# Attention and two expert layers on one core: side steps between the two layers take other places

## The chip, the cores and the metric

The kernel runs on one core of one Trainium2 chip. The metric is the device time of one execution in microseconds (us); lower is better. Times of the trace are us from the start of the profiled span.

## The reference

A linear attention with a decay for each head (batch 2, 8 heads, 768 steps, 64 channels) gives 1536 token rows of 512. Two layers of experts follow, each with 8 experts of 512 x 1024 and 1024 x 512, in which each token goes to the one expert of its largest logit:

```python
# first layer: tokens with x @ w_skip > 0 only
xc = x[do_compute]
logits = xc @ w_gate
e_idx = np.argmax(logits, axis=1)
...
h = np.maximum(xc[mask] @ w1[e], 0.0)
y[mask] = gate_w[mask, None] * (h @ w2[e])
out[do_compute] = xc + y
# second layer: all tokens, at most capacity rows to an expert, in order of tokens
h = np.maximum(np.einsum('ecd,edf->ecf', disp, w1), 0.0)
y = np.einsum('ecf,efd->ecd', h, w2)
out[i] = gate_w[i] * y[expert_idx[i], pos[i]]
```

So the result of the first layer decides to which expert of the second layer a row goes.

## The kernel before

The kernel has an order written out by hand: each engine does its instructions in the order in which the code issues them. Four stages follow each other. Attention runs in six chunks of 128 steps. The first expert layer (weights `w1a`, `w2a`) has for each expert one block of 128 rows. Then comes a passage, in which expert 0 of the second layer (`w1b`, `w2b`) is done in two blocks of 128 rows, since the first of them is known early. Last come experts 1 to 7 of the second layer, each with a pair of blocks.

Products are of float32 split in two parts: `hi` is a rounded copy that ScalarE makes (L252 for weights, 128 x 1024 a piece), `lo` is the rest that VectorE makes (L255). Three products hi x hi, hi x lo, lo x hi give one. In `layer1` and `layer2` a group is six such products of 512 columns (L794); `layer2` is a generator of four groups for the eight blocks of 128 of its middle dimension, and yields after each.

Beside the products runs side work, one step after a group. `step_side()` moves each generator of the list `side` by one step, and then `pump`s: a piece of weights is split (so many as `pieces[0]` says) and loads are issued from SyncE's queue. `site()` does the same for the list `sited`, without a pump. The side work is `route_b`, which routes finished rows of the first layer to experts of the second:

- step 1: the rows are turned by TensorE (L870) and copied by ScalarE (`x2t`, L871);
- step 2: logits (L875), copied by ScalarE (`lgs`, L877);
- step 3: their sum (L881), and on VectorE the choice of the expert (`pick`, from L301 to `m` in L317) and the gate;
- step 4, the rank: how many rows ahead went to the same expert (L329, L330 on TensorE), then on VectorE L901, L903 and the table `whereb` (L907) that holds the slot of each row;
- step 5, the slots: TensorE adds the row numbers to the slots (L343, into `tab`).

The rows of experts 0 to 5 are routed in couples, those of experts 6 and 7 one by one; the couple of experts 4 and 5 is the third couple here, and the generator for expert 7 is called `last`. Ahead of routing, `result` makes the row of an expert (L849 on VectorE, from the accumulator of `layer2`), and within it `write_rows` (L355, from ScalarE's queue) writes the rows to a table in DRAM. When the last slots are known, VectorE casts them to `ids_b` (L1075), and GpSimd gathers the rows of a block from the table (L362). `turned` turns four blocks of 128 by TensorE (L765), and ScalarE and VectorE split the turned block in `hi` and `lo` (`split`, L378 and L379).

Of the kernel before, what the change touches and what calls it, by code (L numbers as in the profile page):

```python
# [16 lines left out]
NT, DM, E, FF = B * S, H * D, 8, 1024  # L17
# [3 lines left out]
FT = FF // 128  # L21
# [20 lines left out]
def kernel(  # L42
# [132 lines left out]
    def idle(n):  # L175
        for _ in range(n):
            yield
# [567 lines left out]
    def psum(tag="t", bufs=3):  # L745
        return ps.tile([128, 512], F32, tag=tag, bufs=bufs, name=tag)
# [13 lines left out]
    def turned(src, g, tag, divided=True):  # L760

        pool = x_p if tag == "x" else m_p
        t = psum()
        for k in range(4):
            nc.tensor.transpose(t[:, 128 * k:128 * k + 128], src[:, 512 * g + 128 * k:512 * g + 128 * k + 128], ident)  # L765
        t = t.rearrange("p (k t) -> p k t", k=4)
        if divided:
            w = 128 if tag == "x" else 256
            hi = pool.tile([128, 4, w], F32R, tag=tag + "h", name=tag + "h")[:, :, 0:128]
            lo = pool.tile([128, 4, w], F32R, tag=tag + "l", name=tag + "l")[:, :, 0:128]  # L770
            split(t, hi, lo)
            return hi, lo
        as_is = pool.tile([128, 4, 128], F32, tag=tag + "w", name=tag + "w", bufs=1)
        nc.scalar.activation(out=as_is, in_=t, func=ACTF.Copy)
        return (as_is,)
# [70 lines left out]
    def result(e, xs, acc):  # L846

        r2 = row2[e // 2 % 2][:, e % 2, :]
        nc.vector.scalar_tensor_tensor(  # L849
            out=r2[:, 0:DM], in0=acc, scalar=xs[:, GCOL:GCOL + 1], in1=xs[:, 0:DM], op0=ALU.mult, op1=ALU.add  # L850
        )
        nc.gpsimd.tensor_copy(out=r2[:, IDCOL:IDCOL + 1], in_=xs[:, IDCOL:IDCOL + 1])
        xs_free.append(xs)

    def route_b(es, lead, rest):


        n, e = len(es), es[0]
        r2 = row2[e // 2 % 2][:, e % 2:e % 2 + n, :]
        there = sm.tile([128, n], F32, tag="there", name="there")  # L860
        nc.gpsimd.tensor_scalar(out=there, in0=r2[:, :, IDCOL], scalar1=0.0, scalar2=None, op0=ALU.is_lt)
        rm = sm.tile([128, n, 8], F32, tag=f"rmb{n}", name="rmb")
        for i in range(n):
            nc.gpsimd.tensor_scalar(out=rm[:, i, :], in0=rev, scalar1=there[:, i:i + 1], scalar2=None, op0=ALU.mult)
        yield from idle(lead)
        x2t = m_p.tile([128, 2, KT, 128], F32, tag="x2t", name="x2t", bufs=1)
        for i in range(n):
            xr = psum()
            for k in range(KT):
                nc.tensor.transpose(xr[:, 128 * k:128 * k + 128], r2[:, i, 128 * k:128 * k + 128], ident)  # L870
            nc.scalar.activation(out=x2t[:, i], in_=xr.rearrange("p (k t) -> p k t", k=KT), func=ACTF.Copy)  # L871
        yield
        lg = psum()
        for k in range(KT):
            nc.tensor.matmul(out=lg[32 * k:32 * k + 32, 0:128 * n], lhsT=wgt[:, k, :], rhs=x2t[:, 0:n, k, :], start=True, stop=True)  # L875
        lgs = sm.tile([128, 256], F32, tag="lgs", name="lgs")
        nc.scalar.activation(out=lgs[:, 0:128 * n], in_=lg[:, 0:128 * n], func=ACTF.Copy)  # L877
        yield
        lt = psum()
        for i in range(n):  # L880
            nc.tensor.matmul(out=lt[:, 8 * i:8 * i + 8], lhsT=lgs[:, 128 * i:128 * i + 128], rhs=zsum[:, 8:16], start=True, stop=True)  # L881
        m, weigh = pick(
            lt[:, 0:8 * n].rearrange("p (a j) -> p a j", a=n), n, 1, rm, r2[:, :, GCOL + 1:GCOL + 2], None, e == E - 1
        )
        if e < E - 1:
            weigh()
        if e >= E - 2:
            write_rows(nc.scalar, r2, n)
        rhs = sm.tile([128, n, 2, 8], BF16, tag=f"rhsb{n}", name="rhsb")
        cu = sm.tile([128, n, 8], BF16, tag=f"cu{n}", name="cu")  # L890
        nc.gpsimd.tensor_copy(out=cu[:, 0, :], in_=cumb)
        for i in range(1, n):
            nc.gpsimd.tensor_tensor(out=cu[:, i, :], in0=cu[:, i - 1, :], in1=m[:, i - 1, :], op=ALU.subtract)
        nc.gpsimd.tensor_scalar(out=rhs[:, :, 0, :], in0=m, scalar1=p1, scalar2=None, op0=ALU.mult)
        for i in range(n):
            nc.gpsimd.tensor_scalar(out=rhs[:, i, 1, :], in0=m[:, i, :], scalar1=float(128 * (NTILE + es[i])), scalar2=None, op0=ALU.mult)
        yield from idle(1 + rest)
        rk = psum()
        ranked(rk, lc[:, 1, :], m.rearrange("p n j -> p (n j)"), cu.rearrange("p n j -> p (n j)"))
        pr = sm.tile([128, n, 8], F32, tag=f"prb{n}", name="prb")  # L900
        nc.vector.tensor_tensor(out=pr, in0=rk[:, 0:8 * n].rearrange("p (a j) -> p a j", a=n), in1=m, op=ALU.mult)  # L901
        sl = sm.tile([128, n], F32, tag=f"slb{n}", name="slb")
        nc.vector.tensor_reduce(out=sl, in_=pr, axis=AX.X, op=ALU.add)  # L903
        where = []
        for i in range(n):
            where.append(sm.tile([128, 257], BF16, tag="whereb", name="whereb"))
            nc.vector.tensor_scalar(out=where[i], in0=iota, scalar1=sl[:, i:i + 1], scalar2=None, op0=ALU.is_equal)  # L907
        if e < E - 2:
            write_rows(nc.scalar, r2, n)
        nc.gpsimd.tensor_tensor(out=cumb, in0=cu[:, n - 1, :], in1=m[:, n - 1, :], op=ALU.subtract)  # L910
        yield from idle(3 if e == E - 2 else 1)
        for i in range(n):
            to_slots(where[i], rhs[:, i], 8, 8)
        yield
# [38 lines left out]
    def site():  # L953

        for g in list(sited):
            try:
                next(g)
            except StopIteration:
                sited.remove(g)

    def step_side():
        for g in list(side):
            try:
                next(g)
            except StopIteration:
                side.remove(g)
        pump(1, pieces[0])

    def run(gen):

        while True:
            try:
                next(gen)
            except StopIteration as stop:
                return stop.value
            step_side()
# [3 lines left out]
    x = x0[0]  # L980
# [28 lines left out]
    second = layer2(h0, "w2a", 0)  # L1009
# [5 lines left out]
    x = turned(xs1[1], 0, "x")  # L1015
    acc = run(second)
    then_route(0, acc)
    for e in range(1, E):
        first = layer1(x, "w1a", e)
        if e == 1:  # L1020
            for _ in range(2):
                next(first)
                step_side()
            x = turned(xs1[2], 0, "x")
        h = run(first)
        if e + 4 < E:
            xs1[e + 4] = gather(ids[:, e + 4:e + 5], 1 + NT)
        elif e == 4:
            gather(ids[:, 8:9], 1 + NT, a0)
        turn = split_T(h, FT, "hT", (True, not whole("w2a", e, 1)))  # L1030
        if e > 1:
            second = layer2(hT.pop(e - 1), "w2a", e - 1)
            next(second)
            step_side()
            site()
            x = turned(xs1[e + 1] if e + 1 < E else a0, 0, "x")
            if e == E - 1:

                for _ in range(2):
                    next(second)  # L1040
                    step_side()
                    site()
                    next(turn)
            acc = last_step(second, FT // 2 - (3 if e == E - 1 else 1))
            then_route(e - 1, acc, step_side)
        site()
        hT[e] = run(turn)
    side += sited
    second = layer2(hT.pop(E - 1), "w2a", E - 1)
    for i in range(FT // 2):  # L1050
        next(second)
        pieces[0] = i < 2
        step_side()
    acc = run(second)
    result(E - 1, xs1[E - 1], acc)
    last = route_b([E - 1], 0, 0)

    xs2 = {(0, 0): a0}
# [6 lines left out]
    for i in range(1, 13):  # L1065
        next(first)
        if i % 3 == 0:
            step_side()
        if i in (2, 4, 5, 9, 12):
            next(last)  # L1070
    try:
        next(first)
# [5 lines left out]
    second = layer2(h0, "w2b", 0)  # L1078
    next(second)
    h0.append(turned(h, 1, "hT"))  # L1080
    acc = run(second)
    while side:
        step_side()
    x = turned(xs2[0, 1], 0, "x")
    pieces[0] = 1
    ct = totals([cum[:, 0, :], cumb])

# [56 lines left out]
    second = layer2(h0, "w2b", 0)  # L1144
# [3 lines left out]
    x = pair_T(1)  # L1148
# [4 lines left out]
    for e in range(1, E):  # L1153
# [4 lines left out]
        if e + 1 < E:  # L1158
            x = pair_T(e + 1)
# [198 lines left out]
```

## Time and profile before

| what | us |
|---|---|
| median of 3 runs | 388.11 |
| lowest and highest run | 387.08, 388.33 |
| the profiled execution | 386.85 |
| its span in the trace | 385.1 |
| TensorE (PE) busy in the span | 369.1 |
| VectorE (DVE) busy | 244.3 |
| ScalarE (ACT) busy | 213.7 |
| GpSimd (POOL) busy | 120.8 |

The span is the part of the execution that the trace shows. PE stands for the products and PEld for the weight loads that overlap them; the ends of products are modelled, so an idle time ahead of an instruction is shown shorter than the pause between two products by the time of a product's flow through the array. Busy times of engines overlap, and their sum is no time of the kernel.

### The profile page before, as it was taken

What the parts mean: (1) busy time and instruction counts of PE and PEld (TensorE: products, weight loads), DVE (VectorE), ACT (ScalarE), POOL (GpSimd) and SP (SyncE); (2) the same over time, 40 slices, a digit from 0 to 9 for tenths busy, and PEclk for the clock granted to TensorE, in tenths of its full rate; (3) what the DMA queues carried; (4) which work ended last, traced back from release to release, by engine and by line L of the source; (5) the groups of instructions that cost most, each with busy time, mean ns of one, the idle gap of its engine ahead of it and who ended that gap; (6) DMA issues with size and microseconds to landing.
All of it is one profiled execution on the core that took longest, in us unless ns stands there. A gap on an engine that the chain in (4) does not pass through costs nothing. (4 is left out here: it accounts for less than half of the span.)

```text
span 385.1 us, 6795 instructions
## 1 busy us (share of the span) xinstructions
PE 369.1 (96%) x2642; PEld 311.0 (81%) x2642; DVE 244.3 (63%) x402; ACT 213.7 (56%) x317; POOL 120.8 (31%) x185
## 2 busy tenths in 40 slices
PE   8999999899999999998899999999999999999992
PEld 4788887687687787875578998989989898998981
DVE  3657776489896988997426993646727376383200
ACT  1446564398878777894227773537536455563100
POOL 3677764284060240403251401305022040401102
PEclk9999999999999999999999999999999999999998
DMA  8999975799999999899434794956749387110101
GB/s 299 416 413 406 361 240 191 234 337 401 382 390 399 381 339 358 295 338 335 168 106 141 270 333 141 307 202 200 260 145 337 114 261 263 56 52 11 43 3 43
DMA packets 18128, 95.99 MB, mean 249 GB/s; under 512 B 2401, under 2 KB 2657, under 8 KB 8616
## 3 DMA queue, kind: packets, MB, share of 16 engines
q1 hardware_dynamic: 12196, 80.85, 57.0%
q0 software_dynamic: 3280, 9.76, 8.0%
q10 hardware_dynamic: 2612, 4.86, 3.3%
q8 instruction: 23, 0.38, 0.4%
q14 instruction: 17, 0.14, 0.1%
HBM read 87.03 MB, written 9.48 MB: 251 GB/s over the span
## 5 line engine op out<-in xcount | busy, mean ns | idle before, releaser
L255 DVE TENSOR_TENSOR lo<-big,hi 128x1024 fp32r<-128x1024 f32 (+1 forms) x130 | 151.2, 1185 | 55.6 <-ACT hi L252 55.2
L252 ACT ACTIVATE hi<-big 128x1024 fp32r<-128x1024 f32 (+1 forms) x130 | 128.5, 1017 | 6.0 <-DMA big<-in_w1a_dram 4.2
L788 PE MATMUL s<-xh,lo 128*128 128x256 f32 x224 | 63.5, 283 | 0.0
L787 PE MATMUL s<-xl,hi 128*128 128x256 f32 x224 | 63.5, 283 | 0.0
L786 PE MATMUL s<-xh,hi 128*128 128x256 f32 x224 | 63.4, 283 | 0.0
L924 POOL DMA_INDIRECT out_dram<-y,ixo x16 | 18.6, 1165 | 139.2 <-ACT y L919 137.5
L786 PE MATMUL o<-hi,hTh 128*128 128x512 f32 x112 | 44.2, 395 | 0.0
L788 PE MATMUL o<-hi,hTl 128*128 128x512 f32 x112 | 43.7, 390 | 0.0
L787 PE MATMUL o<-lo,hTh 128*128 128x512 f32 x112 | 43.6, 390 | 0.0
L786 PEld LDWEIGHTS s<-xh,hi 128*128 128x128 f32 x224 | 43.0, 192 | 0.3
L787 PEld LDWEIGHTS s<-xl,hi 128*128 128x128 f32 x224 | 43.0, 192 | 0.3
L788 PEld LDWEIGHTS s<-xh,lo 128*128 128x128 f32 x224 | 43.0, 192 | 0.0
L1118 ACT ACTIVATE hTh<-s 128x512 fp32r<-128x512 f32 x28 | 16.7, 598 | 39.0 <-PE s L788 38.6
L1119 DVE SCALAR_TENSOR_TENSOR hTl<-s,hTh 128x512 fp32r<-128x512 f32 x28 | 19.3, 690 | 28.4 <-ACT hTh L1118 28.4
L919 ACT ACTIVATE y<-o,rowc 128x512 f32<-128x512 f32 (+1 forms) x15 | 10.1, 674 | 45.4 <-issue 29.3
L794 PE MATMUL s<-hi,xh 128*128 128x512 f32 x80 | 32.7, 409 | 1.6 <-DVE xl L379 0.9
L794 PE MATMUL s<-lo,xh 128*128 128x512 f32 x80 | 31.3, 391 | 0.0
L794 PE MATMUL o<-hi,hTh 128*128 128x512 f32 x72 | 29.7, 413 | 0.0
L794 PE MATMUL o<-lo,hTh 128*128 128x512 f32 x72 | 28.2, 391 | 0.0
L794 PE MATMUL s<-hi,xl 128*128 128x512 f32 x80 | 24.9, 393 | 0.0
L788 PEld LDWEIGHTS o<-hi,hTl 128*128 128x128 f32 x112 | 21.0, 188 | 4.4
L787 PEld LDWEIGHTS o<-lo,hTh 128*128 128x128 f32 x112 | 21.1, 188 | 4.2
(162 smaller groups left out, 603.9 us busy)
## 6 DMA issues: line engine op xcount, KB each, us to landing
big<-in_w1a_dram SPq DMA_DIRECT2D x16, 1024.0 KB, 8.2
big<-in_w2a_dram SPq DMA_DIRECT2D x16, 1024.0 KB, 6.8
big<-in_w1b_dram SPq DMA_DIRECT2D x16, 1024.0 KB, 5.2
big<-in_w2b_dram SPq DMA_DIRECT2D x16, 1024.0 KB, 5.4
qk<-in_qkv_dram SPq DMA_DIRECT2D x5, 1024.0 KB, 10.5
big<-in_qkv_dram SPq DMA_DIRECT2D x5, 1024.0 KB, 13.2
table<-rowc ACTq DMA_DIRECT2D x5, 516.0 KB
table<-row ACTq DMA_DIRECT2D x3, 516.0 KB, 5.3
```

The source lines that it names most:

```text
L252: nc.scalar.activation(out=hi[:, k], in_=r3[:, k], func=ACTF.Copy)
L255: nc.vector.tensor_tensor(out=lo[:, k], in0=r3[:, k], in1=hi[:, k].bitcast(F32), op=ALU.subtract)
L786: nc.tensor.matmul(out=acc, lhsT=a[0], rhs=w[0], start=first, stop=False)
L787: nc.tensor.matmul(out=acc, lhsT=a[0], rhs=w[1], start=False, stop=False)
L788: nc.tensor.matmul(out=acc, lhsT=a[1], rhs=w[0], start=False, stop=last)
L794: nc.tensor.matmul(out=acc, lhsT=a, rhs=w, start=first and i == 0, stop=last and i == len(todo) - 1)
L919: nc.scalar.activation(out=y[:, 0:n], in_=acc[:, 0:n], func=ACTF.Copy, scale=xs[:, GCOL + 1:GCOL + 2])
L924: new = nc.gpsimd.indirect_dma_start(out=out[:, :], out_offset=bass.IndirectOffsetOnAxis(ap=ix, axis=0), in_=y, in_offset=None, bounds_che ...
L1118: nc.scalar.activation(out=hi[:, g:g + 2, :], in_=acc, func=ACTF.Relu)
L1119: nc.vector.scalar_tensor_tensor(out=lo[:, g:g + 2, :], in0=acc, scalar=0.0, in1=hi[:, g:g + 2, :].bitcast(F32), op0=ALU.max, op1=ALU.subtract
```

## The change

Five places between the two layers are written in another order; no instruction is added or taken away.

```diff
-        yield from idle(3 if e == E - 2 else 1)
+        yield from idle(1 if e < E - 4 or e == E - 1 else 3)
         for i in range(n):
             to_slots(where[i], rhs[:, i], 8, 8)
...
             then_route(e - 1, acc, step_side)
-        site()
+        if e < E - 1:
+            site()
         hT[e] = run(turn)
     side += sited
...
     for i in range(FT // 2):
         next(second)
         pieces[0] = i < 2
-        step_side()
+        if i < FT // 2 - 1:
+            step_side()
     acc = run(second)
     result(E - 1, xs1[E - 1], acc)
+    step_side()
     last = route_b([E - 1], 0, 0)
...
-        if i in (2, 4, 5, 9, 12):
+        if i in (2, 4, 5, 8, 12):
             next(last)
...
     h0.append(turned(h, 1, "hT"))
+    for _ in range(FT // 2 - 2):
+        next(second)
+        step_side()
+    x = turned(xs2[0, 1], 0, "x")
     acc = run(second)
     while side:
         step_side()
-    x = turned(xs2[0, 1], 0, "x")
```

The first two edits concern the third couple: its rank is no longer issued right after the products of expert 6, but in the side step behind the first group of expert 7, and its slots three side steps after the rank instead of one. On TensorE, in the second product of experts 6 and 7, the place of the rank of the couple (`m`, 128 x 16) reads so (`o` is the accumulator, `row_1153` the row of expert 6):

```order
 L794 MATMUL o<-hi,hTl 128x512 x2
+L794 MATMUL o<-hi,hTh 128x512
+L794 MATMUL o<-lo,hTh 128x512
+L794 MATMUL o<-hi,hTh 128x512
+L794 MATMUL o<-lo,hTh 128x512
+L794 MATMUL o<-hi,hTl 128x512 x2
+L870 MATMUL t<-cs,row_1153 128x128 x4
 L329 LDWEIGHTS lc
 L329 MATMUL t<-m,lc 128x16
```

The first group of expert 7 and the turn of row 6 now stand ahead of the couple's rank; its eight slots, which stood behind that turn, stand behind the rank of row 6, after the fourth group.

With the third edit the row of expert 7 is made ahead of the last side step of that loop. On VectorE, at the end of the first layer (`o` is the accumulator of expert 7, L901 to L907 the slot table of row 6):

```order
+L849 SCALAR_TENSOR_TENSOR row_1153<-o,rowc_106 128x512
 L901 TENSOR_TENSOR prb<-t,m 128x8
 L903 TENSOR_REDUCE slb<-prb 128x1
 L907 TENSOR_SCALAR whereb<-iota,slb 128x257
-L849 SCALAR_TENSOR_TENSOR row_1153<-o,rowc_106 128x512
```

The row moved ahead of the three instructions of the slot table. The fourth edit puts the rank of row 7 two products of the first expert's first half sooner, ahead of the turn of `h` on TensorE, and so L901 to L907 of row 7 ahead of the split of that turn (L379) on VectorE.

The fifth edit turns the first expert's second block ahead of the fourth group of `layer2`, instead of behind it. On TensorE (`rowc_107` is the gathered block):

```order
-L794 MATMUL o<-hi,hTh 128x512
-L794 MATMUL o<-lo,hTh 128x512
-L794 MATMUL o<-hi,hTh 128x512
-L794 MATMUL o<-lo,hTh 128x512
-L794 MATMUL o<-hi,hTl 128x512 x2
 L765 MATMUL t<-cs,rowc_107 128x128 x4
+L794 MATMUL o<-hi,hTh 128x512
+L794 MATMUL o<-lo,hTh 128x512
+L794 MATMUL o<-hi,hTh 128x512
+L794 MATMUL o<-lo,hTh 128x512
+L794 MATMUL o<-hi,hTl 128x512 x2
```

The turn, which reads the gathered block, moved up by one group of six products.

## Rows read from the trace of the kernel before

**Rows 1.** Busy us (instructions) by stretch: PE, PEld, DVE, ACT, POOL; clock, DMA, GB/s.

```profile
175.00:180.00 5.00, 3.24 (x20) 2.09 (x18) 4.65 (x15) 2.71 (x5) 3.17 (x9) 1.00 0.85 332
260.00:310.00 50.00, 50.00 (x325) 45.82 (x325) 28.76 (x30) 27.52 (x36) 11.21 (x14) 1.00 0.61 207
```

**Rows 2.** What PE waited for, 175 to 215 us: us in total, times, longest.

```profile
PE tab L343 <- DVE whereb L907: 1.4, 2, 0.9
PE t L329 <- DVE m L317: 1.0, 2, 0.7
```

**Rows 3.** Timeline, 175 to 180 us: start, us, instruction [idle before <-releaser].

```profile
175.12 0.62 PE L794 MATMUL o<-hi,hTl 128*128 128x512 f32 x2
...
176.41 0.18 PE L329 MATMUL t<-m,lc 128*128 128x16 bf16 x1 [0.66 <-DVE m L317]
...
176.72 0.37 ACTq L355 DMA_DIRECT2D table<-row  x1
...
177.15 0.74 DVE L849 SCALAR_TENSOR_TENSOR row<-o,rowc 128x512 f32<-128x512 f32 x1
...
178.24 0.60 PE L870 MATMUL t<-cs,row 128*128 128x128 f32 x4
...
178.94 0.60 ACT L871 ACTIVATE x2t<-t 128x512 f32<-128x512 f32 x1 [1.61 <-PE t L870]
...
179.77 0.26 PE L343 MATMUL tab<-rhsb,whereb 128*128 128x8 bf16 x4 [0.93 <-DVE whereb L907]
```

**Rows 4.** Timeline, 179 to 188 us.

```profile
179.43 1.05 ACT L252 ACTIVATE hi<-big 128x1024 fp32r<-128x1024 f32 x1
...
182.21 0.28 ACT L877 ACTIVATE lgs<-t 128x128 f32<-128x128 f32 x1 [1.73 <-PE t L875]
182.38 1.05 ACT L252 ACTIVATE hi<-big 128x1024 fp32r<-128x1024 f32 x1
...
184.61 0.16 DVE L301 TENSOR_REDUCE mx<-t 128x1 f32<-128x8 f32 x1
...
185.70 0.18 PE L329 MATMUL t<-m,lc 128*128 128x8 bf16 x1 [0.36 <-DVE m L317]
...
186.62 0.74 DVE L849 SCALAR_TENSOR_TENSOR row<-o,rowc 128x512 f32<-128x512 f32 x1
...
187.51 0.63 PE L870 MATMUL t<-cs,row 128*128 128x128 f32 x4 [0.58 <-DVE row L849]
```

**Rows 5.** Timeline, 189 to 196 us.

```profile
189.93 0.29 PE L881 MATMUL t<-zsum,lgs 128*128 128x8 f32 x2
...
191.40 0.34 ACTq L355 DMA_DIRECT2D table<-row  x1
...
192.44 0.66 PE L765 MATMUL t<-cs,h 128*128 128x128 f32 x4 [0.29 <-ACT h L817]
...
194.75 0.36 DVE L907 TENSOR_SCALAR whereb<-iota,slb 128x257 bf16<-128x257 f32 x1
...
195.17 0.26 PE L343 MATMUL tab<-rhsb,whereb 128*128 128x8 bf16 x4 [0.46 <-DVE whereb L907]
...
195.92 1.11 POOL L362 DMA_INDIRECT rowc<-table,ids_b  x1 [3.34 <-DVE ids_b L1075]
```

**Rows 6.** Timeline, 199 to 203 us.

```profile
199.96 0.39 PE L794 MATMUL o<-hi,hTh 128*128 128x512 f32 x1
...
201.32 0.60 PE L765 MATMUL t<-cs,rowc 128*128 128x128 f32 x4
...
202.61 0.50 PE L794 MATMUL s<-hi,xh 128*128 128x512 f32 x1 [0.66 <-issue]
```

**Rows 7.** Gathers, issue to landing: by ids_b (second layer), by ids (first layer).

```profile
DMA to landing us min/median/max: 3.9/4.1/5.3
DMA to landing us min/median/max: 3.6/7.6/8.5
```

**Rows 8.** The page's busy tenths of DMA in 40 slices of 9.63 us.

```profile
DMA  8999975799999999899434794956749387110101
```

## Prediction

> **What bounds the kernel now.** I read the busy time by stretch first. From 210 us to the end of the products TensorE is busy without a gap (50.00 of 50 us in each of three stretches there, of which one is shown), at a granted clock of 1.00, while ScalarE and VectorE have 40% of their time free [rows 1]. Nothing in that part can be gained by moving side work, and whatever is gained ahead of it is passed on whole, as long as its weights come in time: TensorE alone paces them there. The stretch that the diff touches is another matter: from 175 to 180 us TensorE is busy for 3.24 of 5 us, and VectorE for 4.65, so there VectorE's queue sets the pace [rows 1]. The list of waits then names what TensorE waits for between 175 and 215 us: for the table of slots `whereb` (1.4 us in two waits) and for the choice of expert `m` (1.0 us in two waits) [rows 2], and the timeline gives the rest with their places: 0.58 us for the last row, and 0.66 us ahead of the first block's second half [rows 4, 6].
>
> So the kernel's time is a chain of TensorE's products and, between 175 and 203 us, five places where it stops. I follow five points of that chain: the turn of row 6 (L870 at 178.24), the rank of row 6 (L329 at 185.70), the turn of row 7 (L870 at 187.51), the last slots (L343 at 195.17), and the first product on the first expert's second block (L794 at 202.61) [rows 3 to 6].
>
> **Units.** A group of six products takes 201.32 - 199.96 = 1.36 us, or 0.23 us each [rows 6]. After VectorE's result of a row TensorE starts 187.51 - (186.62 + 0.74) = 0.15 us later [rows 4].
>
> **1. The third couple's rank a step later.** Before, TensorE issues its last product of the layer at 175.35, is free at 175.6, and stops until the rank at 176.41 [rows 3]. With the rank behind the first group of the next expert, that group runs from 175.6 to 177.0. But next in the queue is now the turn of row 6, which needs VectorE's row, done at 177.15 + 0.74 = 177.89 [rows 3]. The diff leaves VectorE's order up to there as it was, so that time stays. TensorE stops for about 1.1 us and turns the row at 178.05 instead of 178.24: **0.2 us** gained, though a wait of 0.66 us is gone. This is the wait that takes the place of the one removed.
>
> **2. The couple's slots three steps later.** The stop of 0.93 us at 179.77 goes [rows 3], since `whereb` is used some 4 us later. What counts is when the rank of row 6 can start, 7.46 us after the turn before. Two chains lead there. TensorE: turn and rank 0.4, group 1.36, logits 0.4, group 1.36, sum 0.15, group 1.36: 5.0 us. ScalarE and VectorE: the copy of the turned row starts 178.94 - 178.24 = 0.70 us after the turn and takes 0.60 [rows 3]; the couple's write to the table, now behind it in ScalarE's queue, 0.37 [rows 3]; a piece of weights 1.05, the logits' copy 0.28, a second piece 1.05, less some 0.2 for overlaps as between 182.21 + 0.28 and 182.38; from the end of that piece (183.43) VectorE reaches the choice at 184.61, 1.18 later; from there to the rank 1.09 [rows 4]. Sum 6.1 us. The longer one decides, so the rank of row 6 starts at 178.05 + 6.1 = 184.15 instead of 185.70: **1.55 us** gained in all, with a stop of 1.1 us left ahead of it (0.36 before [rows 4]).
>
> **3. Row 7 ahead of the side step.** Behind the rank stand now the couple's eight slots (four took 0.26 us [rows 5]; I take 0.25 for eight, since they overlap) and four products (0.9 us); the row can be turned at 184.15 + 0.1 + 0.25 + 0.9 = 185.4. VectorE's row started 186.62 - 185.70 = 0.92 us after the rank [rows 4], behind three small instructions that read the rank. Now it stands ahead of them: between 0 and 0.92 us after the rank, and I take 0.25, since only the gate's end is left ahead of it. It is done by 184.4 + 0.74 = 185.15, so the stop of 0.58 us [rows 4] goes. Turn at 185.45 instead of 187.51: **2.05 us** in all.
>
> **4. The last rank sooner.** The turn of row 7 to its sum took 189.93 - 187.51 = 2.42 us, and nothing of that moves. The rank now stands four products behind the sum, about when `m` is chosen; a stop of 0.1 us there is covered, since the next turn (L765 at 192.44, 2.51 us behind the sum) waits for ScalarE anyway [rows 5]. The slot table is then made ahead of the split of `h` on VectorE instead of behind it (L907 at 194.75). Without that, TensorE would come to the last slots after the turn, four slots and six products, 0.35 + 0.3 + 1.36 = 2.0 us behind 192.44, that is at 194.45 instead of 195.17: 0.7 us. Last slots at 195.17 - 2.05 - 0.7 = 192.4: **2.75 us** in all.
>
> **5. The second block turned between the third and the fourth group.** Before, 1.29 us pass from the turn (201.32) to the first product (202.61), with 0.66 us of standing still [rows 6]. Now ScalarE's copy lies beside the fourth group: turn 0.35, group 1.36, counts 0.1. That is 1.29 - 0.45 = 0.85 us less, **3.6 us** in all, if the row is there. It comes by a gather, issued 195.92 - 195.17 = 0.75 us after the last slots [rows 5], so at 193.15; the gathers of this table land 3.9 us after issue at the least and 5.3 at the most [rows 7]: 197.05 to 198.45. TensorE comes to the turn at 199.96 - 2.75 = 197.2. Behind the turn stands a group that needs nothing of it, so a late row costs its lateness whole, from 0 to 1.25 us. I take 0, since with few transfers about (3 tenths of DMA time in that slice) the short landings are the nearer ones, and keep 1.25 us for the range. The gather also waits for the table's last write, which ScalarE issues behind the last choice at 191.40 [rows 5]. No row shows its landing; it took less than the 4.52 us that lay between it and the gather. Now 193.15 - (191.40 - 2.05) = 3.8 us lie between, so a late write could cost at most 0.7 us; half a megabyte moves in it, no load is in the queue then, and I take 0.
>
> The order of pumps, and so of weight pieces and loads, is unchanged in number; they move up with TensorE. Sum: 3.6 us (bounds 2.35 with the latest gather; 4.1 if the two stops that I leave at the turn and the rank of row 6 were each a quarter of a us shorter). The profiled execution took 386.85 us, span 385.1, which is 1.26 under the median of 388.11; by it the changed kernel takes 383.2, by the median **384.5**, which I give.
>
> **Rivals.** *Late row.* The gather is the bound at point 5. Landings of 4.3 to 5.3 us give a gain of 2.4 to 3.3 us, so 384.8 to 385.7. For it: the margin is 0.15 us only. Against it: the landings under a light load are the short ones.
>
> *Slower.* The same place decides the other sign. The gathers of the first layer's rows took 7.6 us to land in the median and 8.5 at the most [rows 7], with DMA at 9 tenths [rows 8]. Landing at 193.15 + 8.5 = 201.65, the row would hold up the fourth group too, and the first product would start 1.9 us after that, at 203.55 instead of 202.61: 0.9 us slower, 389.0. It turns slower at a landing of 7.6 us. Against it: DMA stands at 3 to 4 tenths in the slices from 183 to 202 us [rows 8]. The Trainium skill ("DMA: Bandwidth & Descriptors", section "Latency and other measured facts") puts HBM's latency at 0.2 us on average and 2 us under high load, and calls a DMA's fixed cost smaller under lighter load; by it the short landing is to be expected here, and this case's trace agrees (3.9 against 7.6 us).
>
> *Gather held up while it is issued.* One L362 takes about 1.1 us [rows 5]; if VectorE kept GpSimd from writing its descriptors, the row would be late by the time that VectorE works. An L255 of 1.2 us beside it would give a gain of 2.5 us, 385.6. The Trainium skill ("SBUF — State Buffer", section "SBUF: two separate sides") states such a lock for VectorE's two-port modes. In the new order VectorE has nothing between the cast of `ids_b` and the next split of `h`, some 2 us later, so I count this within the late row.
>
> *The rank of row 6 keeps its distance.* If the 7.46 us from row 6's turn to its rank don't shrink, because ScalarE's pieces of weights wait for something that the rows hide, the sum is 0.2 + 0.5 + 0.7 + 0.85 = 2.25 us, 385.9. For it: VectorE's near-full stretch up to 180 us. Against it: ScalarE's copy of logits waited 1.73 us for TensorE [rows 4].
>
> *Without effect.* The later products don't get their weights sooner, so what is gained is given back: 388.1. Against it: both splitting engines have much room there [rows 1].
>
> **Chances.** Forecast 0.68, late row 0.14, rank keeps its distance 0.10, no effect 0.05, slower 0.03. A measurement here can tell 0.3%, 1.16 us, from no change. The first three are faster, but a mix of small losses could fall within the bound: faster 0.88, same 0.08, slower 0.04. The forecast's own range is 383.2 to 385.2 (either base, and 0.7 us of spread as in the three runs). The late row and part of the case with the rank carry the range to 386.3; the lower end is 383.0.
>
> **What would show it.** Right: no wait at the couple's rank and slots; one of about 1.1 us ahead of L870 of row 6 and another of about 1 us ahead of row 6's rank; none ahead of row 7's turn and the last slots; the fourth group directly behind the second block's turn, and the first product directly behind that; from then on every instruction some 3.6 us earlier. Wrong: a stop at the second block's turn until a gather lands, more than 7 us from row 6's turn to its rank, or idle TensorE after 210 us.

## The result, and the profile after

The changed kernel takes 384.49 us in the median of 6 runs (383.41 to 385.04), the kernel before 388.01 us beside it (387.08 to 390.54). The quotient of the two medians is 0.9909; the ratio on record, worked out from the single runs, is 0.9881, with a 95% interval from 0.9849 to 0.9913: about 1% faster. Some executions of the kernels below fell into a slower state (the farthest took 519.55 us), and the ratios, medians and ranges given here leave them out. The profiled execution took 384.92 us, its span 383.1 us.

The busy time by stretch, read as in [rows 1] (us, PE, PEld, DVE, ACT, POOL, clock, DMA share, GB/s). The first two rows are the stretch that the edits touch, from the third couple's sum to the first product on the second block, in the kernel before and in the changed one; the third row is the later stretch in the changed one:

```profile
173.35:202.61 29.26, 25.15 (x152) 18.45 (x150) 14.30 (x44) 9.12 (x18) 10.94 (x25) 1.00 0.60 202
...
174.74:200.43 25.69, 24.37 (x151) 18.14 (x150) 14.91 (x44) 9.08 (x17) 10.19 (x24) 1.00 0.65 227
...
260.00:310.00 50.00, 50.00 (x335) 46.19 (x334) 28.07 (x30) 25.78 (x34) 11.58 (x15) 1.00 0.64 219
```

TensorE's idle time in that stretch fell from 29.26 - 25.15 = 4.11 to 25.69 - 24.37 = 1.32 us (idle times are shown shorter than the pauses, see step 1 below); the later stretch is still full. The row from 175 to 180 us in [rows 1] can't be set beside the same clock times here, since the same work lies 1.39 us later in this execution. What TensorE waited for between 173.5 and 213.5 us is down from the waits of [rows 2], and those of [rows 4, 6] that the prediction added, to two:

```profile
PE t L870 <- DVE row L849: 0.9, 1, 0.9
PE t L329 <- DVE m L317: 0.4, 1, 0.4
```

The timeline shows where (start, us, instruction, in brackets the idle time ahead of it and what ended it). It answers to [rows 3 to 6]; the rows are the ends of the steps, with what stands between them left out.

```profile
174.74 0.51 PE L881 MATMUL t<-zsum,lgs 128*128 128x8 f32 x4
...
177.88 0.61 PE L794 MATMUL o<-hi,hTl 128*128 128x512 f32 x2
...
178.53 0.74 DVE L849 SCALAR_TENSOR_TENSOR row<-o,rowc 128x512 f32<-128x512 f32 x1
...
179.42 0.63 PE L870 MATMUL t<-cs,row 128*128 128x128 f32 x4 [0.92 <-DVE row L849]
...
179.89 0.17 PE L329 MATMUL t<-m,lc 128*128 128x16 bf16 x1
...
180.64 1.06 ACT L252 ACTIVATE hi<-big 128x1024 fp32r<-128x1024 f32 x1
...
182.00 0.28 ACT L877 ACTIVATE lgs<-t 128x128 f32<-128x128 f32 x1 [0.29 <-PE t L875]
182.17 1.05 ACT L252 ACTIVATE hi<-big 128x1024 fp32r<-128x1024 f32 x1
...
184.40 0.16 DVE L301 TENSOR_REDUCE mx<-t 128x1 f32<-128x8 f32 x1
...
184.50 0.62 PE L794 MATMUL o<-hi,hTl 128*128 128x512 f32 x2
...
185.49 0.18 PE L329 MATMUL t<-m,lc 128*128 128x8 bf16 x1 [0.36 <-DVE m L317]
...
185.62 0.75 DVE L849 SCALAR_TENSOR_TENSOR row<-o,rowc 128x512 f32<-128x512 f32 x1
...
186.78 0.60 PE L870 MATMUL t<-cs,row 128*128 128x128 f32 x4
...
189.16 0.29 PE L881 MATMUL t<-zsum,lgs 128*128 128x8 f32 x2
...
193.74 0.25 PE L343 MATMUL tab<-rhsb,whereb 128*128 128x8 bf16 x4
...
194.60 1.11 POOL L362 DMA_INDIRECT rowc<-table,ids_b  x1 [2.67 <-DVE ids_b L1078]
...
198.53 0.60 PE L765 MATMUL t<-cs,rowc 128*128 128x128 f32 x4
198.88 0.48 PE L794 MATMUL o<-hi,hTh 128*128 128x512 f32 x1
...
200.43 0.48 PE L794 MATMUL s<-hi,xh 128*128 128x512 f32 x1
...
375.27 0.39 PE L788 MATMUL o<-hi,hTl 128*128 128x512 f32 x1
```

No idle time stands ahead of the couple's rank (179.89), row 7's turn (186.78), the last slots (193.74), the second block's turn (198.53) or its first product (200.43). Two stops are left, at row 6's turn and ahead of row 6's rank.

Start times of two executions can't be subtracted directly here, since the stretch that no edit touches did not take the same time in both. The last event ahead of all edits is the sum of the third couple's logits (the first L881 above); in the kernel before it stood at 173.35 us, and the last product at 377.50:

```profile
173.35 0.51 PE L881 MATMUL t<-zsum,lgs 128*128 128x8 f32 x4
...
377.50 0.39 PE L788 MATMUL o<-hi,hTl 128*128 128x512 f32 x1
```

So I count all points from that sum. The column "before" comes from [rows 3 to 6] less 173.35, the column "after" from the rows above less 174.74:

| us behind the couple's sum | before | after | gain | predicted |
|---|---|---|---|---|
| turn of row 6 | 4.89 | 4.68 | 0.21 | 0.2 |
| rank of row 6 | 12.35 | 10.75 | 1.60 | 1.55 |
| turn of row 7 | 14.16 | 12.04 | 2.12 | 2.05 |
| last slots | 21.82 | 19.00 | 2.82 | 2.75 |
| first product on the second block | 29.26 | 25.69 | 3.57 | 3.6 |

From that product to the last one pass 377.50 - 202.61 = 174.89 us before [rows 6] and 375.27 - 200.43 = 174.84 us after: the gain is passed on whole. The two spans differ by only 2.0 us, because the couple's sum itself came 1.39 us later in the execution that was profiled after (174.74 against 173.35), and 0.2 us more passed behind the last product. The medians differ by 3.52 us. Why that start moves is told at the end.

### The profile page after: what moved, and what is told of

Same layout as the page of the kernel before. It is cut to its first block, busy times and chain, and to the rows that moved or that the text cites. A ratio compares the mean times of both kernels' runs of the same rounds, so it can differ in the third digit from the quotient of the medians.

```text
span 383.1 us, 6796 instructions
## 1 busy us (share of the span) xinstructions
PE 368.7 (96%) x2641; PEld 311.0 (81%) x2642; DVE 244.7 (64%) x402; ACT 213.8 (56%) x317; POOL 121.1 (32%) x185
## 5 line engine op out<-in xcount | busy, mean ns | idle before, releaser
L255 DVE TENSOR_TENSOR lo<-big,hi 128x1024 fp32r<-128x1024 f32 (+1 forms) x130 | 151.3, 1185 | 54.1 <-ACT hi L252 53.6
```

Of the source, the lines that this page charges most:

```text
L255: nc.vector.tensor_tensor(out=lo[:, k], in0=r3[:, k], in1=hi[:, k].bitcast(F32), op=ALU.subtract)
```

## The experiments

**One part at a time.** Four kernels hold one part of the change each, the rest as before. One execution of the kernel before took 388.07 us beside them.

The third couple's rank and slots later (the first two edits):

```diff
-        yield from idle(3 if e == E - 2 else 1)
+        yield from idle(1 if e < E - 4 or e == E - 1 else 3)
...
-        site()
+        if e < E - 1:
+            site()
```

> Edits 1 and 2 alone (the third couple's rank and slots later). All times count from the third couple's sum (L881). Before, the rank of row 6 starts 12.35 us behind it, the turn of row 7 14.16, the last slots 21.82, the first product on the second block 29.26. Theory: the rank of row 6 at 10.8, with a stop of about 1 us ahead of row 6's turn; row 7's turn is held by its row, 1.8 us behind the rank, so at 12.6; the first product at 27.7, 1.5 us sooner than before. Rival, that the distance from row 6's turn to its rank is fixed by pieces of weights: rank of row 6 at 12.1 and first product at 29.0.

It took 387.94 us. TensorE's timeline at the three turning points:

```profile
180.60 0.63 PE L870 MATMUL t<-cs,row 128*128 128x128 f32 x4 [0.93 <-DVE row L849]
...
186.66 0.18 PE L329 MATMUL t<-m,lc 128*128 128x8 bf16 x1 [0.37 <-DVE m L317]
...
188.57 0.63 PE L870 MATMUL t<-cs,row 128*128 128x128 f32 x4 [0.47 <-DVE row L849]
```

The sum stood at 175.91 us in this execution, so the turn of row 6 came 4.69 us behind it and its rank 10.75, as in the whole change. The first product on the second block stood 27.74 us behind the sum, 1.52 sooner than before. The time of the execution hides that, since its sum came 2.56 us later than in the profiled execution before (175.91 against 173.35): 386.85 + 2.56 - 1.52 = 387.89. The same account gives the times of the three other parts to 0.3 us. The two edits of the couple were not run apart; of the 1.60 us at row 6's rank the points put 0.21 ahead of row 6's turn, where the couple's rank is out of the way, and the rest behind it, where its slots are.

Row 7 ahead of the side step (the third edit):

```diff
-        step_side()
+        if i < FT // 2 - 1:
+            step_side()
     acc = run(second)
     result(E - 1, xs1[E - 1], acc)
+    step_side()
```

> Edit 3 alone (the row of expert 7 ahead of the last side step). Theory: the rank of row 6 stays at 12.35 us behind the couple's sum; row 7 is made right behind the choice, the turn of row 7 stands at 13.4 instead of 14.16, and the first product on the second block at 28.5, 0.75 us sooner. Rival, that the row is not ready sooner because VectorE still has the accumulator or the gate to wait for: turn at 14.1 and no gain.

It took 386.97 us. The stop ahead of the rank of row 6 is there as before, the one ahead of row 7's turn is gone:

```profile
186.60 0.18 PE L329 MATMUL t<-m,lc 128*128 128x8 bf16 x1 [0.35 <-DVE m L317]
...
187.67 0.60 PE L870 MATMUL t<-cs,row 128*128 128x128 f32 x4
```

With its sum at 174.25 us, row 7 is turned 13.42 us behind it (14.16 before), and the first product comes 28.48 behind it: 0.78 us gained.

The last rank sooner (the fourth edit):

```diff
-        if i in (2, 4, 5, 9, 12):
+        if i in (2, 4, 5, 8, 12):
```

> Edit 4 alone (the last rank two products sooner). Theory: the turn of row 7 stays at 14.16 us behind the couple's sum; the last slots come 6.95 us behind that turn instead of 7.66, without a stop; the first product on the second block at 28.55, 0.7 us sooner. Rival, that TensorE's stop for m at the earlier place costs what the later place gave: last slots 7.4 us or more behind the turn, gain under 0.3 us.

It took 388.0 us. The last slots no longer wait for `whereb`:

```profile
196.10 0.26 PE L343 MATMUL tab<-rhsb,whereb 128*128 128x8 bf16 x4
```

They stand 21.14 us behind the sum (174.96), 21.82 before, and the first product 28.57: 0.69 us gained.

The second block turned amid the products (the fifth edit):

```diff
+    for _ in range(FT // 2 - 2):
+        next(second)
+        step_side()
+    x = turned(xs2[0, 1], 0, "x")
     acc = run(second)
...
-    x = turned(xs2[0, 1], 0, "x")
```

> Edit 5 alone (the second block turned between the third and the fourth group). Theory: everything up to the last slots as before (21.82 us behind the couple's sum); first product 6.6 us behind the last slots instead of 7.44, so 0.85 us sooner, and no stop at the turn, which stands about 4.0 us behind the gather's issue. Rival, that the gather is late: TensorE stops ahead of the turn and the first product comes 6.9 to 7.9 us behind the last slots.

It took 386.92 us. From the last slots at 195.73 us to the first product pass 6.69 us (202.61 - 195.17 = 7.44 before [rows 5, 6]):

```profile
200.52 0.60 PE L765 MATMUL t<-cs,rowc 128*128 128x128 f32 x4
...
202.42 0.48 PE L794 MATMUL s<-hi,xh 128*128 128x512 f32 x1
```

The gain is 0.75 us. The four single gains, 1.52, 0.78, 0.69 and 0.75, add up to 3.74 us; together the five edits give 3.57. The parts are nearly independent. Most of the rest lies at row 7's turn: the stop there is 0.58 us before [rows 4], but 0.47 us once the couple is moved, so the row's own move has less to remove.

**How close is the gather?** The second block's turn was moved up by another group in the changed kernel.

```diff
-    for _ in range(FT // 2 - 2):
+    for _ in range(FT // 2 - 3):
```

> The changed kernel, with the second block turned between the second and the third group, so that TensorE comes to the turn about 2.6 us behind the gather's issue. It measures the landing. Theory (landing 3.6 to 3.9 us after issue, seen by the profile of the changed kernel): TensorE stops at the turn for 1.0 to 1.4 us, the turn starts 3.7 to 4.0 us behind the issue, and the first product comes 7.6 to 8.0 us behind the last slots instead of 6.7. Rival, that the landing is well below what the profile counts (some 2.6 us, when the bytes have moved): no stop, and the first product as in the changed kernel.

It took 386.38 us, with the kernel before at 389.87 us in the median on that chip. GpSimd's issue and TensorE's turn and first product:

```profile
195.03 1.11 POOL L362 DMA_INDIRECT rowc<-table,ids_b  x1 [2.54 <-DVE ids_b L1078]
...
198.59 0.63 PE L765 MATMUL t<-cs,rowc 128*128 128x128 f32 x4 [0.73 <-DMA rowc<-table,ids_b]
...
201.88 0.48 PE L794 MATMUL s<-hi,xh 128*128 128x512 f32 x1
```

Now the transfer is the bound: TensorE starts 3.56 us after the issue, a little sooner than the 3.7 to 4.0 that I expected, behind a stop of 0.73 us. In the changed kernel it comes to the same turn 198.53 - 194.60 = 3.93 us after the issue, without a stop. The margin there is therefore some 0.4 us. A row that is late costs its lateness whole, as the prediction said: the first product stands 26.57 us behind this execution's sum (175.31), against 25.69, 0.88 us later. One group sooner is the right place, two are too many.

**Room that is left.** Both remaining stops wait for VectorE, which splits pieces of weights (L255) between the steps of the routing. Here one piece of the last wide product is split later, behind the choice of row 6.

```diff
-        pieces[0] = i < 2
+        pieces[0] = i < 1
...
     result(E - 1, xs1[E - 1], acc)
+    pieces[0] = 1
     step_side()
+    pieces[0] = 0
```

> The changed kernel, with the piece of weights that stands ahead of row 6's choice on ScalarE and VectorE moved behind the last side step of that loop. Theory (the chain of ScalarE and VectorE sets row 6's rank): the choice starts about 0.7 us sooner, the rank of row 6 comes with TensorE at about 10.1 us behind the couple's sum instead of 10.75, its stop of 0.36 us is gone, and all that follows is 0.6 us sooner: 383.9 by the changed kernel's median. Rival, that row 6's rank is bound by something else: rank at 10.75, no gain; or that the piece then delays row 7's choice: row 7's chain (turn to sum 2.4 us) gets longer by up to 1 us.

It took 385.58 us in the median, 0.9877 of the kernel before, from 0.982 to 0.9934. The stop ahead of the rank is gone and the rank stands 10.23 us behind the sum (175.43) instead of 10.75, 0.52 us sooner; the first product stands 25.25 behind it, a gain of 0.44 us. By the ratios the times of the two kernels can't be told apart. The 0.1 us that is missing went at the gather. The busy time from 190 to 193 us, in this kernel and in the changed kernel, shows a load beside the table's last write, since the moved piece frees its buffer later (the load is issued at 188.50 us here, right behind the moved L255, and at 184.51 in the changed kernel; last columns: DMA share, GB/s):

```profile
190.00:193.00 3.00, 2.97 (x20) 1.98 (x19) 1.42 (x9) 1.28 (x3) 0.85 (x3) 1.00 0.89 346
```

```profile
190.00:193.00 3.00, 2.97 (x20) 1.99 (x19) 1.38 (x9) 1.35 (x3) 0.85 (x3) 1.00 0.46 173
```

The write then landed 3.6 us after its issue instead of 3.1, and the gather was issued 1.27 us after the last slots instead of 0.86. In the nine other profiles it is issued 0.74 or 0.75 us after them, and in the five of these that have the write's landing it took 2.3 to 2.5 us. So the gather seems to wait for the write in these two profiles, though its idle time is put down to the cast of `ids_b`. This is the late write to which the prediction gave 0.7 us at most.

**Two pieces later.** On top of that, one piece is split behind row 6's turn instead of ahead of it, and one behind the issue of the gathers.

```diff
-                for _ in range(2):
+                for i in range(2):
                     next(second)
+                    pieces[0] = i < 1
                     step_side()
...
+                pieces[0] = 1
...
         load_block(e, j)
+    pump(1, 1)
```

> As the kernel before this one, and the piece ahead of the third couple's choice is also moved back, so that each later piece moves by one step and the last is split behind the cast of the last slots. Theory (VectorE's queue, not the row itself, makes row 6 late for its turn): the couple's choice starts about 1 us sooner, row 6's turn stands at about 3.7 us behind the couple's sum instead of 4.68, without the stop of 0.92 us, row 6's rank at about 9.1 to 9.3, and all that follows 1.5 us sooner than in the changed kernel: 383.0. Rival, that the pieces only change places: VectorE is then late at row 6's choice or at the split of the first expert's turned half, and the gain is 0.6 us or less.

It took 385.61 us in the median, 0.9908 of the kernel before, from 0.9868 to 0.9948. In its profile the turn of row 6 stands 4.15 us behind the sum (176.42), not at the 3.7 that I expected, and the first product 24.61, 1.08 us sooner than in the changed kernel and not 1.5. That did not show in the time, so the changed kernel and this one were timed beside each other on one chip, with a new profile of each.

> The changed kernel itself, timed beside the version with two pieces moved. Expected 384.5 us, 0.988 of the kernel before; the points counted from the third couple's sum as in its first profile, the first product on the second block 25.7 us after that sum and 174.8 us from there to the last product. If the stretch up to the couple's sum, which no edit touches, spreads from execution to execution as it did (173.4 to 176.4 us in nine profiles), its place in this profile can lie anywhere in that range.

> The version with two pieces of the last wide layer moved behind the choices of rows 6 and 7. If the 1.08 us by which its first product came sooner in its profile are real and passed on, its median lies about 1.1 us under the changed kernel's on the same chip, near 383.4 us or 0.985 of the kernel before; if the spread of the start decides, the two medians can't be told apart, while the point of the first product counted from the couple's sum is again near 24.6 us against 25.7.

The changed kernel took 386.38 us in the median (382.82 to 387.13), 0.9923 of the kernel before, from 0.9886 to 0.9959; that is nearer to 1 than the 0.9881 of its first runs, and the two intervals overlap. The one with two pieces moved took 384.68 us (382.73 to 386.18), 0.989, from 0.9857 to 0.9924. By the ratios the step between the two is not settled, since their intervals overlap. The medians lie 1.70 us apart, and all 11 runs with the pieces moved, but 4 of 10 of the changed kernel, took at most 386.18 us. The profiles agree with the first ones to 0.03 us. The changed kernel, its sum and its first product (25.66 us apart):

```profile
176.14 0.51 PE L881 MATMUL t<-zsum,lgs 128*128 128x8 f32 x4
...
201.80 0.48 PE L794 MATMUL s<-hi,xh 128*128 128x512 f32 x1
```

The version with two pieces moved (24.62 us apart):

```profile
173.49 0.51 PE L881 MATMUL t<-zsum,lgs 128*128 128x8 f32 x4
...
175.51 0.60 ACT L378 ACTIVATE hTh<-t 128x512 fp32r<-128x512 f32 x1 [0.61 <-PE o L794]
...
177.64 0.63 PE L870 MATMUL t<-cs,row 128*128 128x128 f32 x4 [0.39 <-DVE row L849]
...
193.20 1.23 DVE L255 TENSOR_TENSOR lo<-big,hi 128x1024 fp32r<-128x1024 f32 x1 [1.31 <-ACT hi L252]
193.59 1.72 POOL L362 DMA_INDIRECT rowc<-table,ids_b  x1 [0.30 <-issue]
...
198.11 0.48 PE L794 MATMUL s<-hi,xh 128*128 128x512 f32 x1
```

Counted from the sum, the order saves 1.04 us. ScalarE's split of the turned half (L378) now waits 0.61 us for TensorE, and VectorE's row comes behind that split: the pieces of weights no longer hold row 6, though TensorE still stops for the row (0.39 us).

## Why the prediction was right

The forecast, 384.5 us, met the median of 384.49. That they meet so closely is luck, since the start of the kernel moves by 3.1 us from one execution to the next, and the same kernel took 386.38 us on another chip. What carries the account is that the five points met their steps to 0.07 us. Most of that rests on one reading: that from 210 us on only TensorE paces the kernel [rows 1], so that a step ahead of it counts whole. It held to 0.1 us in all eleven profiles: from the first product on the second block to the last product pass 174.8 to 174.9 us. "Without effect" fell with it.

**Step 1.** The wait of 0.66 us [rows 3] was exchanged for one at row 6's turn. TensorE was free of the group at 177.88 + 2 x 0.23 = 178.34 and turned the row at 179.42: 1.08 us, forecast 1.1. The row shows 0.92, since idle times ahead of a product are shown shorter than the pause.

**Step 2.** The turn of row 6 to its rank took 185.49 - 179.42 = 6.07 us, forecast 6.1, and 7.46 before. That is the end of "the rank keeps its distance". Three sizes in it were off. TensorE's own path took 184.50 + 0.46 - 179.42 = 5.54 us, forecast 5.0, mostly since a group that begins behind a product of another kind took 1.47 to 1.56 us instead of 1.36; so the stop ahead of the rank is 0.53 us by the starts (0.36 shown) and not 1.1. This had no effect on the sum, since the other chain is the longer one. The two other sizes lie on that longer chain, and that they nearly cancel is luck: the logits' copy did wait for TensorE, by 0.29 us, so up to there TensorE's queue set the pace and not ScalarE's, while the couple's write, counted at 0.37 us, took none of ScalarE's time between the copy of the row and the first piece (180.64). The second piece ended at 183.22, and from there the choice came 1.18 us later and the rank 1.09 after that, both as read from [rows 4].

**Step 3.** VectorE's row started 0.13 us after the rank, within the bounds of 0 and 0.92 and nearer to 0 than the 0.25 taken. The turn came 1.29 us after the rank, forecast 1.3, without a stop. The part alone gave 0.78 us.

**Step 4.** Row 7's turn to its sum took 2.38 us (2.42 before), and the last slots came 4.58 us behind the sum, 195.17 - 189.93 = 5.24 before [rows 5]: 0.66 us, forecast 0.7, and 0.69 alone.

**Step 5.** The term was mis-sized by 0.1 us: 0.75 us for 0.85, alone and with the rest. From the turn to the first product pass 1.90 us with a group in it, forecast 0.35 + 1.36 + 0.1 = 1.81; the group behind the turn is again one of the longer ones. The gather held. Its own landing is not in the changed kernel's trace; those of the four that are issued behind it took

```profile
DMA to landing us min/median/max: 3.6/3.7/3.9
```

after their issues (3.9 at the least in [rows 7]). The gather itself was there 3.56 us after its issue with the turn another group sooner, and landed after 3.4 us in the first two profiles with pieces moved; so the margin was some 0.4 us and not 0.15. The landings of 5 us and more, on which the late row and the slower rival rested, did not come at this place. The Trainium skill ("DMA: Bandwidth & Descriptors", section "Latency and other measured facts") calls the fixed cost smaller under lighter load; the trace agrees, with 3.7 us in the median at a DMA share of 0.51 (194 to 204 us) against 7.6 us for the first layer's gathers [rows 7], at shares of up to 9 tenths [rows 8]. The late write, taken at 0, cost 0.11 us at the issue (0.86 us behind the slots, 0.75 in [rows 5]) and nothing at the turn; the write moves 258 KB, and not the half megabyte that the prediction says.

**The gather held up while it is issued.** In the changed kernel the first issue took 1.11 us with nothing on VectorE, so this rival had no place. What it rests on does occur, though: in the version with two pieces moved, the second gather's issue took 1.72 us, in both profiles, where an L255 had started 0.39 us ahead of it (193.20 and 193.59 above), and 1.00 us without one. The Trainium skill ("SBUF — State Buffer", section "SBUF: two separate sides") states a lock between VectorE with two SBUF inputs and a GpSimd operation that reads SBUF, for the whole instruction; by it L362 would wait for the 0.84 us that were left of L255, and the trace shows 0.72 more. The first layer's gathers show the same in all eleven profiles; in the changed kernel:

```profile
81.20 1.23 DVE L255 TENSOR_TENSOR lo<-big,hi 128x1024 fp32r<-128x1024 f32 x1
...
81.83 1.46 POOL L362 DMA_INDIRECT rowc<-table,ids  x1 [0.30 <-issue]
...
86.77 0.68 DVE L379 TENSOR_TENSOR xl<-t,xh 128x512 fp32r<-128x512 f32 x1
...
87.05 1.03 POOL L362 DMA_INDIRECT rowc<-table,ids  x1 [0.16 <-issue]
```

An L255 with 0.60 us left made the issue 0.46 us longer than 1.00. An L379 with 0.40 us left, which reads only one of its two inputs from SBUF (`t` lies in PSUM), made it 0.03 us longer. What a held issue costs its own landing is open: the gather of 1.72 us landed 6.6 us after its issue in the first profile with two pieces moved, but a load of weights ran beside it.

## What to carry to other kernels

Where one engine is full to the end, follow its order as a chain of a few named points and ask at each which of two paths arrives last; a removed wait then shows up as the next one, and its price can be read before the edit is made. Count the points from the last event that no edit touches: here the start of the kernel moved by nearly as much as the change was worth, and neither the spans nor single times showed the parts. Ahead of a transfer, move its reader one group at a time, since a late transfer costs its whole lateness in a full queue.

## What was not expected of the hardware

The same instructions up to the couple's sum ended between 173.35 and 176.42 us in eleven profiled executions, 3.1 us apart, though no edit of any of these kernels touches what stands ahead of it. I can name three sources, not the share of each in every execution.

The first is the clock at the start. In three executions the granted clock was 0.50 or 0.51, the lower of the two levels, from 10 to 15 us, and the first rank (L329) stood at 21.98 to 22.31 us; in the others it was 1.00 there and the rank stood at 19.90 to 21.31. A window of one of the three (the couple alone):

```profile
10.00:15.00 5.00, 5.00 (x52) 4.78 (x52) 1.83 (x7) 1.34 (x3) 2.83 (x6) 0.50 0.99 411
```

It fell in the second of two stops of TensorE (the granted clock was 0.69 in the mean from 8.5 to 9 us, 0.50 from 9 to 10):

```profile
7.90 0.46 PE L624 MATMUL s<-qk 64*128 64x128 f32 x2 [0.45 <-PE s L624]
8.97 2.04 PE L624 MATMUL s<-qk 64*128 64x128 f32 x14 [0.62 <-DVE mask L575]
```

In the turn alone the same two stops, of 0.45 and 0.62 us, stood 0.3 us sooner and the clock stayed at 1.00; what decides is open.

The second is a gather near 72 us that TensorE waits for in some executions (0.30 to 1.07 us shown) and not in others; the changed kernel's first profile has

```profile
71.89 0.71 PE L372 MATMUL m<-cs,a 128*128 128x128 f32 x4 [0.62 <-DMA a<-table,ids]
```

The third is a load of weights near 118 us. ScalarE waits for it in front of the copy that TensorE needs, so that TensorE's wait is put down to ScalarE; it ranged from none to the 1.40 us of the last rank alone:

```profile
118.55 1.06 ACT L252 ACTIVATE hi<-big 128x1024 fp32r<-128x1024 f32 x1 [3.08 <-DMA big<-in_w1a_dram]
119.52 1.07 ACT L871 ACTIVATE x2t<-t 128x512 f32<-128x512 f32 x2
...
120.64 0.64 PE L875 MATMUL t<-x2t,wgt 128*32 128x256 f32 x8 [1.40 <-ACT x2t L871]
```
